# Last column loop: block 15 scored straight from PSUM with x weighted in advance, its last half block cut in two, and two middle half blocks summed by VectorE

## The chip, the cores and the metric

One core of one Trainium2 chip. The time is the device time of the whole program in microseconds (us). The kernel before was run three times; the trace that is read here is of one further, profiled execution.

## The reference, cut to what matters

For each of four batches, a long convolution over 12,608 positions and 128 channels (done here by matmul transforms) gives `y`, and `x * y` is the attention output. Then a top-k step replaces 128 rows of each batch:

```python
attn_out = x * y                                   # [4, 12608, 128]
scores = np.einsum('bsd,d->bs', attn_out, w_gate)
out = attn_out.copy()
for b in range(B):
    top_idx = np.argpartition(-scores[b], 128)[:128]
    xe = attn_out[b, top_idx]
    ye = np.maximum(xe @ w1, 0.0) @ w2
    g = 1 / (1 + np.exp(-scores[b, top_idx]))
    out[b, top_idx] = attn_out[b, top_idx] + g[:, None] * ye
```

So every row needs its product `x * y`, which goes to the output, and a score, the sum over 128 channels of that product times the gate vector `w_gate`.

## The kernel before, in words

Most of the program is a software pipeline over 128 groups (4 batches of 32), which transforms `u = x * v`, multiplies by the filter's spectrum and transforms half way back. What the change touches is the second half of the way back, the **column loop** `P1.run(ex)`, and only for the last batch, where nothing else is left in the pipeline (`ex` is set, `self.last` is true). For the other batches `P1` runs with `ex` empty.

A batch is 128 columns `j` of 128 rows by 128 channels. They are cut in 16 blocks of 8 columns, taken in the order `ORD` (0, 8, 1, 9, ... 7, 15), and each block in two half blocks of 4 columns: `hbs`, numbered `h` = 0 to 31. Half blocks 30 and 31 are block 15. Blocks 8 to 15 are called far here, the others near. For each `h` the loop emits

- `mm(h)`: the matmuls of its columns into one of three PSUM banks in turn (names `a`, `a`, `c` in the trace; lines 539 and 543). A bank can be written again when the half block three earlier has been read.
- `fin(h)`: VectorE multiplies the bank by `x` in SBUF, in place, into `xa` (line 554, 512 columns). Then the pending half block is weighted by the gate vector (`weigh`, line 589): near ones on VectorE, one half block later, with the gate vector held in PSUM; far ones on GpSimd at once (except `DW`). ScalarE sums the weighted products, one Copy with an accumulator for each column (`sums`, line 599). For `h` = 30 and 31 (`end`) VectorE does the scores itself with four multiply-and-accumulate operations (line 572), after the pending weighting.
- at the end of a block: the DMA of `xa` to the output (line 579; ScalarE's queue for the blocks at places 2 to 9 of the order, SyncE's for the others), a load of `x` for the block eight places on into the room of the block before (`load_a`, line 516, SyncE's queue, which must wait until that room's output DMA has landed; the load of block 15, at place 15, is emitted when the block at place 8, half blocks 16 and 17, is done), and after blocks 1 to 5 a `comb` on GpSimd (line 526), which prepares a near block's columns.

After the loop come the mask (line 603, VectorE) and the top-k of the last batch: 16 rounds, each of which counts on VectorE and ScalarE, adds up the counts with small matmuls (`total`, bf16, into a fourth bank) and makes a step on VectorE. The expert matmuls of the three other batches are woven in. `ex.start()`, emitted ahead of round 0, issues on TensorE in this order: the first half of an expert's first layer into the first bank of the ring (line 281, 16 rows in the trace), the second half into the second bank, and eight warming matmuls (line 811) into the third; on ScalarE a relu of the first half. Each engine runs its instructions in the order of emission.

Of the kernel before, what the change touches and what calls it, by code (L numbers as in the profile page):

```python
# [12 lines left out]
ALU = mybir.AluOpType  # L13
# [4 lines left out]
B, S, D, FO = 4, 12608, 128, 64  # L18
# [11 lines left out]
HB = 4  # L30
# [20 lines left out]
PC = 8  # L51
NL, NM = 28, 7
DW = (2, 14)
XI = 3
OFF, _o = {}, 0
for _n, _k, _w in (("te", 2, 2 * HC), ("qs", 2, HC), ("mt", 1, 2 * HC), ("ws", 1, 888), ("yz", 2, 2 * HC), ("sd", 2, 2 * HC),
# [5 lines left out]
CE = [o + 8 * D for o in XE]  # L62
XP = [OFF["wx"][0], *(OFF["xa"][0] + k * 8 * D for k in range(NX))]
XP[XI:XI] = XE
EARLY = [k for k in range(len(XP)) if not XI <= k < XI + 2]
KH = N1 // 2 + 1
# [113 lines left out]
def hyena_moe(ctx, tc, xg, x2, pos, bw, ww, wg, mw1, mw2, fo, fc, c1, gx, cf, ci, wm, tk, out):  # L180
    nc = tc.nc
# [6 lines left out]
    arena = cp.tile([128, ARENA], F32, name="arena")  # L188
    big = cp.tile([128, D * 2 * NJ + 4], F32, name="big")

    def view(t, off, shape):
        n = int(np.prod(shape[1:]))
        r = t[:shape[0], off:off + n]
        if len(shape) > 2:
            ax = "abcd"[:len(shape) - 1]
            r = r.rearrange(f"p ({' '.join(ax)}) -> p {' '.join(ax)}", **dict(zip(ax[1:], shape[2:])))
        return r
# [5 lines left out]
    def small(shape, name, dt=F32, tag=None):  # L203
        return sp.tile(shape, dt, tag=tag, name=name, bufs=2 if tag == "sc" else 1)
# [10 lines left out]
    def ps2(k, shape, name):  # L215
        return view(bank2[k], 0, shape)
# [18 lines left out]
    wgb = cp.tile([128, D + 4], F32, name="wgb")[:, 2:2 + D]  # L235
# [5 lines left out]
    junk = view(arena, OFF["cm"][0] + 2 * NC * D, [128, D])  # L241
# [25 lines left out]
    def stage_u(t):  # L267
        if t >= B * NG:
            return
        x, v = buf("x", t, [NP, XC]), buf("v", t, [NP, XC])  # L270
        nc.gpsimd.tensor_tensor(out=x, in0=x, in1=v, op=ALU.mult)  # L271
# [159 lines left out]
    def f_m(t, uv):  # L431
        ht = slots[:, t].rearrange("p (w c) -> p w c", w=2) if t < NG else buf("ht", t, [128, 2, HC])
        mt = buf("mt", t, [128, 2, HC])
        nc.vector.tensor_tensor(out=mt, in0=uv, in1=ht[:, 0].unsqueeze(1).to_broadcast([128, 2, HC]), op=ALU.mult)  # L434
        nc.vector.tensor_tensor(out=uv, in0=uv, in1=ht[:, 1].unsqueeze(1).to_broadcast([128, 2, HC]), op=ALU.mult)  # L435
        return mt

    def f_y(t, uv, mt):
        yz = buf("yz", t, [128, 2, HC])
        nc.vector.tensor_tensor(out=yz[:, 0], in0=uv[:, 1], in1=mt[:, 0], op=ALU.add)  # L440
        nc.vector.tensor_tensor(out=yz[:, 1], in0=mt[:, 1], in1=uv[:, 0], op=ALU.subtract)
        return yz
# [54 lines left out]
    hbs = [(ja, min(HB, z - ja)) for a, z in (blocks[k] for k in ORD) for ja in range(a, z, HB)]  # L497

    class P1:
        def __init__(self, b):  # L500
            self.b = b
            self.sc = small([128, NJ], f"sc_{b}", tag="sc")
            self.xa, self.s4, self.cm = {}, {}, {}
            self.mul = None
            self.hbs = hbs
            self.more = iter(CB)
            self.pw = self.nw = 0
            self.late = []
# [37 lines left out]
        def fin(self, h):  # L546
            ja, n = self.hbs[h]
            blk = ja // 8
            xa = self.xa[blk]
            js = slice(ja % 8, ja % 8 + n)  # L550
            end = self.last and h >= len(self.hbs) - 2
            if end:
                self.weigh()
            nc.vector.tensor_tensor(out=xa[:, js], in0=self.s4.pop(h)[:, :n], in1=xa[:, js], op=ALU.mult)
            if not end:
                self.weigh()
                far = ja >= JM and h + 1 < len(self.hbs) and h not in DW
                if h >= NL and not self.last:
                    o = OFF["cm"][0] + 2 * NC * D if h < 30 else OFF["wx"][0]
                    wx = view(arena, o + h % 2 * HB * D, [128, HB, D])  # L560
                elif far:
                    wx = view(arena, CE[self.pw % 2], [128, HB, D])
                    self.pw += 1
                else:
                    wx = self.wx[self.nw % len(self.wx)]
                    self.nw += 1
                self.mul = xa[:, js], wx[:, :n], ja, n, far, h
                if far:
                    self.weigh()
            else:  # L570
                for k in range(n):
                    nc.vector.scalar_tensor_tensor(out=junk, in0=xa[:, ja % 8 + k], scalar=1.0,
                                                   in1=self.wg, op0=ALU.mult, op1=ALU.mult,
                                                   accum_out=self.sc[:, ja + k:ja + k + 1])
            if ja + n == blocks[blk][1]:
                j0, j1 = blocks[blk]
                i = ORD.index(blk)
                eng = nc.scalar if 1 < i <= len(ORD) - len(XP) + 1 else nc.sync
                eng.dma_start(out[self.b, :, j0:j1], xa[P0:P0 + PR, :j1 - j0])
                if i:  # L580
                    self.load_a(i - 1 + len(XP))
                if blk in CB:
                    self.comb()

        def weigh(self):
            if self.mul:
                x, wx, ja, n, far, h = self.mul
                eng, w = (nc.gpsimd, wgb) if far else (nc.vector, self.wg)
                eng.tensor_tensor(out=wx, in0=x, in1=w.unsqueeze(1).to_broadcast([128, n, D]), op=ALU.mult)  # L589
                cols = [(wx[:, k], ja + k) for k in range(n)]  # L590
                if h < NL or self.last:
                    self.sums(cols)
                else:
                    self.late += cols
            self.mul = None
# [9 lines left out]
        def run(self, ex):  # L605
            self.last = ex is not None
            self.ring = (0, 1, 2) if ex else (3, 2, 0, 1)
            o = OFF["te"][0], OFF["ht"][0] + ((self.b + 1) * NG + 2) % NH * 2 * HC, OFF["x"][0] + (NU - 1) * XC
            if ex:
                o = OFF["te"][0] + 2 * HC, OFF["sd"][0], OFF["sd"][0] + 2 * HC  # L610
            self.wx = [view(arena, k, [128, HB, D]) for k in o]
            self.wg = ps2(1, [128, D], f"wg_{self.b}")
            nc.scalar.copy(out=self.wg, in_=wgb)
            for k in range(len(XE)):
                self.load_a(XI + k)
            for k in range(2):
                self.comb()
            for h in range(len(self.hbs)):
                self.mm(h)
                self.fin(h)  # L620
                if h == 29:
                    stage_u((self.b + 1) * NG + 5)
                if ex:
                    ex.hook(h, self.wg)
            self.weigh()
            if ex:
                self.mask()
# [465 lines left out]
    ex = None  # L1093
    bg = Background(iter(()))
    NT = B * NG
    for t in range(NT + LAG):
# [4 lines left out]
        if t < NT:  # L1101
# [19 lines left out]
            o = t - 1 in uv  # L1121
            if o:
                y = f_y(t - 1, uv[t - 1], f_m(t - 1, uv.pop(t - 1)))
# [23 lines left out]
        if t == NT:  # L1147
            bg.now = t
            bg.drain()
            ex = Experts(picked)  # L1150
# [8 lines left out]
        if i >= 0 and i % NG in LA:  # L1159
            if i % NG == LA[0]:  # L1160
                ph[b] = P1(b)
            k, e = divmod(LA.index(i % NG), 2)
# [39 lines left out]
def build(inputs):  # L1202
    import concourse.bacc as _bacc
    nc = _bacc.Bacc("TRN2", target_bir_lowering=False, num_devices=1, dynamic_dma_scratch_size=4096)
    arrays, args = {}, []
    for name, a in _layout(inputs):
        arrays[f"in_{name}_dram"] = a
        args.append(nc.dram_tensor(f"in_{name}_dram", a.shape, mybir.dt.from_np(a.dtype), kind="ExternalInput").ap())
    args.append(nc.dram_tensor("out_0_dram", (B, PR, NJ, D), F32, kind="ExternalOutput").ap())
    with tile.TileContext(nc) as tc:  # L1210
        hyena_moe(tc, *args)
    return nc, arrays
# [7 lines left out]
```

## Time and profile before

| | us |
|---|---|
| median of 3 runs | 829.29 |
| the runs | 828.87, 829.29, 840.53 |
| profiled execution | 828.99 |
| its span, first to last instruction | 827.2 |
| of it, the last column loop and the mask | 745.6 to 786.5 |
| 16 top-k rounds | 786.6 to 809.8 |
| selection, gather, last expert, scatter | 809.8 to 827.2 |

Busy shares over the whole span are TensorE 97%, VectorE 86%, GpSimd 79% and ScalarE 75%. They are means over stages with different limits; the change lies in one stage of some 40 us, so the stage is what is read. Times in the rows are us from the start of the span. A number in brackets at the end of a row is the idle time before it, with what ended it. Busy times of successive operations overlap a little, so the price of one is the distance between starts.

### The profile page before, as it was taken

Reading aid. Unit: us, or ns where it says so; the run is one execution under the profiler, and the core shown is the slowest. Engines: PE = TensorE matmul, PEld = TensorE weight load, DVE = VectorE, ACT = ScalarE, POOL = GpSimd, SP = SyncE. Lnnn points to the kernel's source line nnn. Section 1 sums busy time; section 2 is a strip of 40 time slices with the busy share of each in tenths; the row PEclk is TensorE's granted clock in tenths of the full one; section 3 lists DMA queues with packets and bytes.
Section 4 is the critical chain, followed back from the end, with each engine's and each line's share of the span. In section 5 each row is a group of like instructions: output and inputs, shape, how many; then the busy total and the mean of one; then the engine's idle time right before and its main releaser. Section 6 shows DMA issues by size and latency. Waiting matters only on the chain.

```text
span 827.2 us, 45233 instructions
## 1 busy us (share of the span) xinstructions
PE 802.9 (97%) x19216; PEld 675.9 (82%) x19216; DVE 712.4 (86%) x1402; ACT 616.7 (75%) x2273; POOL 654.9 (79%) x772
## 2 busy tenths in 40 slices
PE   9999999999999999999999999999999999999975
PEld 8989677777799777778998777778997777979864
DVE  7488899999899898999988989888989989997873
ACT  5366686555579898976599898856798989767971
POOL 5100499999998898999997999989988999989610
PEclk9999999999999999999999999999999999999996
DMA  8100577678969766787788666777797667846800
GB/s 285 43 2 2 186 222 220 219 244 273 290 207 346 246 213 208 231 271 260 229 289 319 216 213 203 254 232 241 250 328 243 218 213 231 268 148 208 321 29 7
DMA packets 77851, 178.41 MB, mean 216 GB/s; under 512 B 9104, under 2 KB 43897, under 8 KB 77649
## 3 DMA queue, kind: packets, MB, share of 16 engines
q1 hardware_dynamic: 73552, 161.23, 60.7%
q10 hardware_dynamic: 3840, 13.76, 4.9%
q8 instruction: 151, 2.47, 1.2%
q0 software_dynamic: 256, 0.52, 0.2%
q14 instruction: 52, 0.42, 0.1%
HBM read 135.77 MB, written 39.71 MB: 212 GB/s over the span
## 4 chain that ended last, share of the span: by engine, by line
PE 82%; DVE 5%; ACT 4%; DMA 2%; issue 2%; POOL 2%; SPq 1%; POOLq 0%; DVEq 0%; ACTq 0%
PE c L285 23%; PE a L420 18%; PE c L290 17%; PE a L539 6%; PE c L543 6%; PE c L539 3%; PE f L390 3%; PE a L374 3%; ACT arena L599 2%; PE f L356 2%; PE a L543 1%; DMA arena<-in_pos_dram 1%; PE a L356 1%; DMA arena<-hd 1%; DVE arena L434 1%
## 5 line engine op out<-in xcount | busy, mean ns | idle before, releaser
L285 PE MATMUL c<-ci_sb,arena 128*23 128x128 f32 x8128 | 249.2, 272 | 1.2 <-issue 0.6
L285 PEld LDWEIGHTS c<-ci_sb,arena 128*23 128x23 f32 x8128 | 226.6, 103 | 10.7 <-issue 2.5
L447 POOL TENSOR_TENSOR arena<-arena 128x364 f32<-128x364 f32 x127 | 113.8, 896 | 97.3 <-PE a L420 70.1
L290 PE MATMUL c<-arena,cf_sb 128*32 128x364 f32 x2048 | 185.5, 470 | 3.2 <-issue 1.5
L420 PE MATMUL a<-cons,arena 128*32 128x182 f32 (+1 forms) x4096 | 186.5, 318 | 1.2 <-POOL big L494 0.9
L420 PEld LDWEIGHTS a<-cons,arena 128*32 128x32 f32 (+1 forms) x4096 | 132.4, 110 | 50.3 <-issue 23.5
L599 ACT ACTIVATE arena<-arena 128x128 f32<-128x128 f32 x504 | 148.0, 299 | 9.7 <-DVE arena L589 9.2
L422 ACT COPY arena<-a 128x364 f32<-128x364 f32 x256 | 119.3, 466 | 43.7 <-PE a L420 39.3
L476 ACT COPY big<-c 128x768 f32<-128x768 f32 x127 | 100.2, 789 | 64.4 <-PE c L285 57.8
L271 POOL TENSOR_TENSOR arena<-arena 128x508 f32<-128x508 f32 x128 | 139.3, 1088 | 2.5 <-DMA arena<-in_xg_dram 2.5
L448 POOL TENSOR_TENSOR arena<-arena 128x364 f32<-128x364 f32 x127 | 114.3, 900 | 0.0
L290 PEld LDWEIGHTS c<-arena,cf_sb 128*32 128x32 f32 x2048 | 69.3, 110 | 48.6 <-issue 41.5
L599 ACT ACTIVATION_READ_ACCUMULATOR arena<-arena 128x1 f32 x504 | 96.2, 191 | 0.0
L429 DVE TENSOR_TENSOR c<-c,arena 128x364 f32<-128x364 f32 x128 | 69.6, 544 | 24.9 <-ACT arena L293 23.5
L434 DVE TENSOR_TENSOR arena<-c,arena 128x728 f32<-128x728 f32 x95 | 86.9, 914 | 2.8
L494 POOL TENSOR_TENSOR big<-big,arena 128x252 f32<-128x252 f32 x128 | 80.5, 629 | 10.0
L435 DVE TENSOR_TENSOR c<-c,arena 128x728 f32<-128x728 f32 x95 | 86.8, 914 | 0.0
L493 POOL TENSOR_TENSOR big<-big,arena 128x252 f32<-128x252 f32 x128 | 80.8, 632 | 1.0 <-ACT arena L477 1.0
L440 DVE TENSOR_TENSOR arena<-c,arena 128x364 f32<-128x364 f32 x127 | 68.2, 537 | 13.2 <-POOL arena L271 0.5
L293 ACT COPY arena<-c 128x364 f32<-128x364 f32 x128 | 59.2, 463 | 18.0 <-PE c L290 8.3
L426 DVE TENSOR_TENSOR c<-c,arena 128x364 f32<-128x364 f32 x128 | 69.6, 544 | 2.7
L526 POOL TENSOR_TENSOR arena<-big 128x512 f32<-128x512 f32 x56 | 70.3, 1281 | 0.7 <-PE c L539 0.6
(222 smaller groups left out, 1294.5 us busy)
## 6 DMA issues: line engine op xcount, KB each, us to landing
arena<-in_xg_dram SPq DMA_DIRECT2D x256, 254.0 KB, 3.3
arena<-hd SPq DMA_DIRECT2D x96, 364.0 KB, 4.2
arena<-in_x_dram SPq DMA_DIRECT2D x40, 420.0 KB, 6.2
out_dram<-arena SPq DMA_DIRECT2D x32, 420.0 KB, 5.8
out_dram<-arena ACTq DMA_DIRECT2D x32, 420.0 KB, 6.3
hd<-big SPq DMA_DIRECT2D x32, 364.0 KB, 3.8
arena<-in_x_dram SPq DMA_DIRECT2D x48, 210.0 KB, 4.5
arena<-in_pos_dram SPq DMA_DIRECT2D x8, 364.0 KB, 6.4
```

Of the source, the lines that this page charges most:

```text
L271: nc.gpsimd.tensor_tensor(out=x, in0=x, in1=v, op=ALU.mult)
L285: nc.tensor.matmul(o[32 * k:32 * k + c.stop - c.start], lhsT=lhsT[:, c], rhs=rhs, start=True, stop=True)
L290: nc.tensor.matmul(pq[a:a + 32, w], lhsT=cf_sb[:, 2 * w + a // NQ, a % NQ:a % NQ + 32], rhs=te[:, a // NQ], start=True, stop=True)
L420: nc.tensor.matmul(tps[s // 2][c, s % 2], lhsT=u[:, s, c], rhs=c1_sb[:, k], start=True, stop=True)
L422: nc.scalar.copy(out=te[:, :, 2 * h:2 * h + 2].rearrange("p e s i -> p s e i"), in_=tps[h])
L434: nc.vector.tensor_tensor(out=mt, in0=uv, in1=ht[:, 0].unsqueeze(1).to_broadcast([128, 2, HC]), op=ALU.mult)
L435: nc.vector.tensor_tensor(out=uv, in0=uv, in1=ht[:, 1].unsqueeze(1).to_broadcast([128, 2, HC]), op=ALU.mult)
L447: eng.tensor_tensor(out=nat(sd[:, 0]), in0=nat(yz[:, 0]), in1=rev(yz[:, 1]), op=ALU.add)
L448: eng.tensor_tensor(out=nat(sd[:, 1]), in0=rev(yz[:, 0]), in1=nat(yz[:, 1]), op=ALU.subtract)
L476: nc.scalar.copy(out=ay[:, t % NG, :NJ + JM, ss], in_=o3[:, :, :NJ + JM].rearrange("p s x -> p x s"))
L493: nc.gpsimd.tensor_tensor(out=d, in0=a, in1=s, op=ALU.subtract)
L599: nc.scalar.activation(out=x, in_=x, func=AF.Copy, accum_out=self.sc[:, j:j + 1])
```

## The change

It works on the last column loop alone (`ex` set).

- `hbs[-1]`, four columns, is cut in two half blocks of two columns, so that the loop has 33 half blocks, and 30, 31 and 32 are block 15.
- `ahead`: GpSimd multiplies `x` of half blocks 30, 31 and 32 by the gate vector, after `fin(25)`, `fin(26)` and `fin(27)`, into rooms of their own (`xw`).
- `fin` of 30 to 32: VectorE no longer multiplies into `xa`. It scores from PSUM, `sum(bank * xw)`, one operation for each column. ScalarE copies the bank to SBUF (`y`), GpSimd multiplies `y` by `x` into `xa`, and the output DMA follows.
- `DS`: for half blocks 17 and 21 (near) VectorE does the scores itself with four multiply-and-accumulate operations, in place of one weighting on VectorE and four sums on ScalarE.

```diff
+DS = (17, 21)
...
-            end = self.last and h >= len(self.hbs) - 2
+            end, ps = h in self.xw, self.s4.pop(h)[:, :n]
             if end:
                 self.weigh()
-            nc.vector.tensor_tensor(out=xa[:, js], in0=self.s4.pop(h)[:, :n], in1=xa[:, js], op=ALU.mult)
-            if not end:
+                for k in range(n):
+                    nc.vector.scalar_tensor_tensor(out=junk, in0=ps[:, k], scalar=1.0, in1=self.xw[h][:, k], op0=ALU.mult,
+                                                   op1=ALU.mult, accum_out=self.sc[:, ja + k:ja + k + 1])
+                y = self.ys[h]
+                nc.scalar.copy(out=y, in_=ps)
+                nc.gpsimd.tensor_tensor(out=xa[:, js], in0=y, in1=xa[:, js], op=ALU.mult)
+            else:
+                nc.vector.tensor_tensor(out=xa[:, js], in0=ps, in1=xa[:, js], op=ALU.mult)
+            if self.last and h in DS:
+                self.weigh()
+                for k in range(n):
+                    nc.vector.scalar_tensor_tensor(out=view(arena, OFF["v"][0] + 16, [128, D]), in0=xa[:, ja % 8 + k],
+                                                   scalar=1.0, in1=self.wg, op0=ALU.mult, op1=ALU.mult,
+                                                   accum_out=self.sc[:, ja + k:ja + k + 1])
+            elif not end:
                 self.weigh()
...
-            else:
-                for k in range(n):
-                    nc.vector.scalar_tensor_tensor(out=junk, in0=xa[:, ja % 8 + k], scalar=1.0,
-                                                   in1=self.wg, op0=ALU.mult, op1=ALU.mult,
-                                                   accum_out=self.sc[:, ja + k:ja + k + 1])
...
+        def ahead(self, h, o, y):
+            ja, n = self.hbs[h]
+            self.xw[h], self.ys[h] = (view(arena, a, [128, HB, D])[:, :n] for a in (o, y))
+            nc.gpsimd.tensor_tensor(out=self.xw[h], in0=self.xa[ja // 8][:, ja % 8:ja % 8 + n],
+                                    in1=wgb.unsqueeze(1).to_broadcast([128, n, D]), op=ALU.mult)
...
+            if ex:
+                ja, n = hbs[-1]
+                self.hbs = hbs[:-1] + [(ja, n // 2), (ja + n // 2, n - n // 2)]
+                v, y = OFF["v"][0] + 16, XP[0]
+                rooms = {25: (30, CE[1] + HB * D, y), 26: (31, v, y + HB * D), 27: (32, v + 2 * D, y + (HB + 2) * D)}
             for h in range(len(self.hbs)):
                 self.mm(h)
                 self.fin(h)
+                if ex and h in rooms:
+                    self.ahead(*rooms[h])
```

## Rows read from the trace of the kernel before

**Rows 1.** The chain that ended last, 700 to 830 us: start, length, what.
```profile
773.04 11.46 ACT arena L599 x79
...
784.57 1.65 ACT arena L599 x11
786.25 0.29 DVE sc L603
```

**Rows 2.** Timeline of TensorE: half block 21, half blocks 30 and 31, then the rounds.
```profile
770.09 1.04 PE L543 MATMUL a<-big,cons 128*64 128x128 f32 x16
...
780.13 1.92 PE L539 MATMUL a<-big,cons 128*64 128x128 f32 x32
782.94 1.09 PE L281 MATMUL a<-arena 128*64 128x128 f32 x16 [0.89 <-issue]
784.88 1.09 PE L281 MATMUL a<-arena 128*64 128x128 f32 x16 [0.85 <-DVE arena L554]
785.91 2.05 PE L811 MATMUL c<-ident 128*128 128x128 f32 x16
788.10 0.26 PE L281 MATMUL c<-st,onesb 128*64 128x3 bf16 x6
```

**Rows 3.** Timeline of VectorE: half blocks 18 and 21, then 28 to 31.
```profile
768.48 0.69 DVE L554 TENSOR_TENSOR arena<-a,arena 128x512 f32<-128x512 f32 x1
...
771.64 0.69 DVE L554 TENSOR_TENSOR arena<-a,arena 128x512 f32<-128x512 f32 x1 [0.64 <-PE a L539]
...
780.96 1.27 DVE L589 TENSOR_TENSOR arena<-arena,c 128x512 f32<-128x512 f32 x2
782.15 0.68 DVE L554 TENSOR_TENSOR arena<-a,arena 128x512 f32<-128x512 f32 x1
782.94 0.29 DVE L572 SCALAR_TENSOR_TENSOR arena<-arena,c 128x128 f32<-128x128 f32 x1
...
784.14 0.69 DVE L554 TENSOR_TENSOR arena<-a,arena 128x512 f32<-128x512 f32 x1
```

**Rows 4.** Timeline of GpSimd: the weightings of half blocks 22 and 23, 26 and 27.
```profile
774.41 2.16 POOL L589 TENSOR_TENSOR arena<-arena,wgb 128x512 f32<-128x512 f32 x2
778.16 2.26 POOL L589 TENSOR_TENSOR arena<-arena,wgb 128x512 f32<-128x512 f32 x2 [1.59 <-ACT arena L599]
```

**Rows 5.** Timeline of SyncE's queue, 773 to 775 us: the load of block 15.
```profile
773.88 0.33 SPq L516 DMA_DIRECT2D arena<-in_x_dram  x1
```

**Rows 6.** Operations on `in_x_dram`, 750 to 790 us: the eight loads of the loop, to landing.
```profile
DMA to landing us min/median/max: 4.4/6.2/7.9
```

**Rows 7.** Source line 516, 773.5 to 774.2 us: the load of block 15, to landing.
```profile
DMA to landing us min/median/max: 6.2/6.2/6.2
```

**Rows 8.** Timeline of all engines, 781 to 792 us: the first relu after the sums, rounds 0 and 1.
```profile
786.12 0.57 ACT L980 ACTIVATE arena<-a 128x512 f32<-128x512 f32 x1
...
788.40 0.16 DVE L728 SCALAR_TENSOR_TENSOR st<-c,cons 128x3 f32<-128x3 f32 x1 [0.21 <-PE c L281]
...
789.90 0.16 DVE L728 SCALAR_TENSOR_TENSOR st<-c,cons 128x3 f32<-128x3 f32 x1 [0.53 <-ACT arena L717]
```

**Rows 9.** Stretches of 1 us: length, busy us (count) of PE, PEld, DVE, ACT, POOL; granted clock; DMA share, GB/s.
```profile
804.00:805.00 1.00, 0.02 (x1) 0.00 (x0) 0.84 (x7) 0.80 (x3) 0.07 (x1) 0.89 0.19 66
...
812.00:813.00 1.00, 1.00 (x7) 0.98 (x8) 0.96 (x5) 0.00 (x0) 0.00 (x0) 0.50 0.00 0
...
818.00:819.00 1.00, 0.33 (x1) 0.14 (x1) 0.00 (x0) 0.23 (x1) 0.00 (x0) 0.78 0.00 0
...
825.00:826.00 1.00, 0.00 (x0) 0.00 (x0) 0.00 (x0) 0.00 (x0) 0.00 (x0) 0.63 0.19 66
```

**Rows 10.** Timeline of TensorE after 800 us: last dense matmuls ahead of a fall, warming at the half clock.
```profile
801.10 1.10 PE L281 MATMUL c<-arena 128*64 128x128 f32 x16
...
814.20 3.78 PE L811 MATMUL a<-ident 128*128 128x128 f32 x16
...
820.02 2.79 PE L281 MATMUL c<-arena 128*64 128x128 f32 x48
```

More of the change, by code (lines that the diff above doesn't have):

```diff
@@ L502, in __init__ @@
             self.sc = small([128, NJ], f"sc_{b}", tag="sc")
-            self.xa, self.s4, self.cm = {}, {}, {}
+            self.xa, self.s4, self.cm, self.ys = {}, {}, {}, {}
             self.mul = None
             self.hbs = hbs
+            self.xw = {}
             self.more = iter(CB)
```

## The prediction

> **What bounds the kernel now.** I read the chain of waits first, for the stretch that the change touches: it shows who hands over to the top-k. Up to about 773 us it runs through the column loop's matmuls, and from there on through ScalarE: 79 and then 11 rows of its sums, one after the other, until VectorE's mask starts at 786.25 [rows 1]. Each sum has two rows, so these 45 sums took 11.46 + 1.65 = 13.1 us, 0.29 each. Four sums are 1.17 us for a half block.
>
> Then each engine's timeline. VectorE ends its last score at almost the same moment: four scores start at 782.94 and the next product at 784.14, 0.30 a score, and four more follow the product of half block 31 [rows 3]. So two engines finish together, and a gain needs both to finish earlier. TensorE has ended the loop's matmuls long before, at 780.13 + 1.92 = 782.05. It then runs what `ex.start()` has put ahead of round 0, as its banks come free: one half layer at 782.94, as soon as VectorE's product of half block 30 has been read out (782.15 + 0.68), the second at 784.88 after the product of 31, then the warming matmuls [rows 2, 3]. These end at 785.91 + 2.05 = 787.96, and round 0's total starts at 788.10 [rows 2]. This is the row to keep in mind: TensorE reaches the first total 0.14 us before it is wanted. Whatever delays the two half layers delays the top-k one for one. What follows the second half layer takes 788.10 - 784.88 = 3.22, and the half layer itself 785.91 - 784.88 = 1.03; from the start of the first to the total it is 4.25 us without a hole.
>
> **The parts, and where each lies.**
>
> *Removed at the end.* VectorE loses the products of 30 and 31, at some 0.6 each (two operations of that width in 1.27, [rows 3]). The eight scores stay: still one operand in PSUM and one in SBUF, so I keep 0.3 each. Alone, this ends VectorE some 1.2 us earlier.
>
> *Half blocks 17 and 21.* ScalarE loses eight sums, 2.35 us. VectorE gets four scores (1.2) for one weighting (0.6) each time, but all four stand ahead of the next product. The product of 18 then moves from 768.48 to about 769.7 and ends at 770.4. TensorE needs the bank for half block 21 at 770.09 [rows 2], so it waits 0.35 us, and about 0.3 more at 25, after the scores of 21. VectorE has a hole of 0.64 us ahead of product 21 [rows 3], and one like it at each second near half block, which swallows the rest. The loop's matmuls end at 782.7 instead of 782.05, and VectorE's last score at about 785.45.
>
> *The weighting ahead on GpSimd.* Here the price is large. `ahead(30)` stands in GpSimd's queue after `fin(25)`, and behind it stand the weightings of 26 and 27, for whose results ScalarE waits. It reads `x` of block 15. That block's load is issued at 773.88 [rows 5], the last of eight on SyncE's queue, since it waits for room. It lands 6.2 us after its issue [rows 7]: at 780.1. Before, nobody wanted it ahead of 782.15. GpSimd has weighted 22 and 23 at 774.41 + 2.16 = 776.6 [rows 4], in the changed kernel some 0.7 later, at 777.3, and would then stand still for 2.8 us. The eight loads landed after 4.4 to 7.9 us [rows 6]; with the shortest it would still be 778.3, with the longest 781.8.
>
> From 780.1 on: `ahead(30)` 1.09 (half of the two in 2.16, [rows 4]), weighting 26 1.09, `ahead(31)` about 0.6 for half the width (an estimate from the same row), weighting 27 1.09, that is 784.0. Before, weighting 27 was through at 778.16 + 2.26 = 780.4 [rows 4]. ScalarE, which is through with 25 and 26 by then, does the sums of 27, 28 and 29 after it: 12 x 0.29 = 3.5, end at 787.5, where before it ended at 786.2. The eight sums saved are more than lost in waiting.
>
> *The copies on ScalarE.* The first, of bank 30, stands behind the sums of 29. It is as wide as the relu of 0.57 us [rows 8], also from PSUM, so it ends at 788.1. The next two are half as wide and hide behind the first half layer.
>
> *Who waits for them.* The half layers write the banks of 30 and 31, which are now free when ScalarE has copied them, no longer when VectorE has read them. The first starts at 788.15 instead of 782.94. Round 0's total follows 4.25 us later: 792.4 instead of 788.1, **+4.3**. The mask (787.6) and VectorE's 1.85 us from there to the counts (788.10 - 786.25) are hidden behind that. In round 1 VectorE waited 0.53 us for ScalarE, which was late by a relu [rows 8]; the relu is now done in time. That gives back between 0 and 0.53; I take 0.25, since part of the hole would be there anyway.
>
> *The clock.* TensorE now stands idle from 782.7 to 788.15, 5.4 us. Twice the trace shows the granted clock fall from 1.00 to 0.50 (2.4 to 1.2 GHz) after dense matmuls end: they end at 802.2 and the clock is down within 804 to 805, and they end at 822.8 and it is down within 825 to 826, 2.5 to 2.6 us later [rows 9, 10]. This gap is twice that, and nothing runs in it. At the half clock the 16 warming rows take 3.78 us instead of 2.05, 1.84 times as long [rows 2, 10]. The clock came back at about 818.4, some 6 us after the matmuls had become dense at 812 [rows 9]. So a fall costs between 0 (it doesn't come) and 4.25 x 0.84 = 3.6 us (the whole chain at the half clock). With 6 us at the half level it would be 6 x 0.46 = 2.8; the stretch after 812 was not without holes and the half layers are, so I take 5 us, **+2.3**.
>
> *Edits with no cost.* GpSimd's products for the output (1.09 and twice 0.6 after the copies) and the last output DMA move to about 790.5, and some 7 us of transfer follow. Behind them on GpSimd stands the first scatter (its turn came at 791.4 and shifts with the rounds), on SyncE nothing; the gather that reads the output comes after 815. One more half block is no more matmuls.
>
> **Sum.** Against the profiled execution of 828.99 (the median of the runs is 829.29, 0.3 more): 828.99 + 4.3 - 0.25 + 2.3 = **835.4 us**. The rounds and all that follows only shift.
>
> **The rivals.**
>
> 1. *The clock holds.* Everything else as above: 833.1. For it: only two falls are seen, and both were followed by thin or no work, so what comes after is not the same. Against it: 5.4 us idle. Chance 0.2.
> 2. *GpSimd isn't stopped by the load* (it lands by 777.3, against the shortest of eight). Then `ahead` fits in GpSimd's hole of 1.59 us [rows 4]. ScalarE still waits some 1.8 us for 18 and 22, since VectorE's four scores delay these products, and ends at 785.7 rather than 2.35 earlier; the first half layer starts at 786.25, the total 4.25 later, at 790.5: +2.4 - 0.25, so 831.1. With an idle TensorE of 3.5 us the clock may fall too, 833.4 then. Chance 0.15.
> 3. *Not slower: the change gives what it takes off VectorE and ScalarE.* The half layers would have to be out of the way, and the load in time. Then the mask starts at 785.75, 0.5 earlier, and with the 0.25 of round 1 it is 828.3. Against it: the matmuls that overwrite the banks have to wait for the copies, and the rows show no slack. It decides from a total wanted later than TensorE is ready. Chance 0.07.
> 4. *VectorE and GpSimd get in each other's way.* GpSimd's three products for the output, 2.3 us in all, now fall beside the mask and the first top-k operations, which have two inputs in SBUF. If such operations wait for each other, VectorE's counts come up to 2.3 us later. In the forecast this stays hidden: 787.6 + 1.85 + 2.3 = 791.8, ahead of TensorE's 792.4. Where TensorE is not the last (rival 3) it turns the gain into 828.3 + 2.3 = 830.6. No row shows such an operation beside a tensor operation of GpSimd. Chance 0.05. The Trainium skill (SBUF — State Buffer, section "SBUF: two separate sides") speaks for this rival: it calls the port pair that VectorE and GpSimd share "an exclusive lock, not a bandwidth split", which a VectorE operation with two SBUF inputs and a GpSimd operation can't hold together. No run here shows it yet.
>
> **How the numbers follow.** The forecast has 0.53. The range goes from 830.6 (rivals 2 and 4) to 836.8 (the forecast with the whole 3.6 for the clock); left out are rival 3 and some tail, about 0.15. A change of 2%, 16.6 us, is about what a measurement of this kernel can tell from none; none of the cases comes near it: faster 0.0, same 0.99, slower 0.01 for a collision that I haven't seen.
>
> **What would show it.** Right: GpSimd idle for 2 to 3 us ahead of `ahead(30)`, released by the load; ScalarE's sums end at about 787.5; the first half layer is released by ScalarE's copy at about 788; round 0's total starts at 792 to 796; a granted clock of 0.50 somewhere between 785 and 795. Wrong: GpSimd runs `ahead(30)` before 779, or the half layers start before the copies, or the clock stays at 1.00. The load is the step I am least sure of, since its landing moves with what the queues do.

## The result

The changed kernel takes **835.83 us** (median of 8 runs, 833.88 to 839.16), the kernel before, run beside it, 831.13 (8 runs). The ratio is **1.007, with a 95% interval of 1.0046 to 1.0094**: some 4 to 8 us slower. The forecast was 835.4, in a range of 830.6 to 836.8.

The profiled execution took 838.06 us, 9.1 more than the one of before. Not all of this need belong to the change: the column loop's first matmul starts at 750.11 us there and at 745.61 before, in code that is the same up to that point. The two rows are from the timelines of TensorE, before and after:

```profile
745.61 0.44 PE L539 MATMUL a<-big,cons 128*64 128x128 f32 x4 [0.61 <-ACT big L476]
```

```profile
750.11 0.44 PE L541 MATMUL a<-big,cons 128*64 128x128 f32 x4 [0.62 <-ACT big L477]
```

So in what follows every time is also given from the loop's first matmul on, written **L+**. Before, round 0's total comes at 788.10 - 745.61 = L+42.49, and the span ends at L+81.6; after, the total comes at 797.72 - 750.11 = **L+47.61** and the end at L+86.2. What the change costs in these two executions, 5.1 us, is all there at the first total, and 4.6 is left at the end.

The chain that ended last, 760 to 840 us, for the stretch of [rows 1]:

```profile
786.75 0.59 POOL arena L598
787.34 1.05 POOL arena L605
788.42 1.92 ACT arena L615 x13
...
790.68 1.35 ACT arena L615 x9
792.03 0.48 ACT arena L560
792.56 3.25 PE a L282 x32
795.81 1.98 PE c L834 x16
```

Before, it ran from ScalarE's sums to VectorE's mask. Now it begins on GpSimd (line 598 is `ahead`, 605 the weighting), goes on to ScalarE's last sums (615) and its copy of a bank (560), and from there to TensorE: the two half layers (282) and the warming (834). VectorE isn't on it any more. GpSimd's timeline, for [rows 4]:

```profile
779.84 2.15 POOL L605 TENSOR_TENSOR arena<-arena,wgb 128x512 f32<-128x512 f32 x2
784.61 1.09 POOL L598 TENSOR_TENSOR arena<-arena,wgb 128x512 f32<-128x512 f32 x1 [2.62 <-DMA arena<-in_x_dram]
785.66 1.09 POOL L605 TENSOR_TENSOR arena<-arena,wgb 128x512 f32<-128x512 f32 x1
786.71 0.64 POOL L598 TENSOR_TENSOR arena<-arena,wgb 128x256 f32<-128x256 f32 x1
787.30 1.09 POOL L605 TENSOR_TENSOR arena<-arena,wgb 128x512 f32<-128x512 f32 x1
```

`ahead(30)` waits 2.62 us for the load of `x`, and the two weightings stand behind it. TensorE's timeline, for [rows 2]:

```profile
792.56 3.25 PE L282 MATMUL a<-arena 128*64 128x128 f32 x32 [5.25 <-ACT arena L560]
795.74 2.05 PE L834 MATMUL c<-ident 128*128 128x128 f32 x16
797.72 0.26 PE L282 MATMUL c<-st,onesb 128*64 128x3 bf16 x6
```

An idle time of 5.25 us, ended by ScalarE's copy; the two half layers (32 rows) in 3.25 us. The granted clock in stretches of 1 us, as [rows 9]:

```profile
791.00:792.00 1.00, 0.00 (x0) 0.00 (x0) 0.00 (x0) 1.00 (x9) 0.00 (x0) 0.91 0.00 0
792.00:793.00 1.00, 0.44 (x4) 0.45 (x6) 0.88 (x4) 1.00 (x4) 0.36 (x1) 0.50 0.00 0
...
795.00:796.00 1.00, 1.00 (x14) 0.83 (x11) 0.51 (x5) 1.00 (x7) 0.32 (x1) 0.89 0.00 0
```

It falls to 0.50 shortly before the half layers begin and is back before the warming ends. Last, VectorE from the mask (line 619) on, with the wait of rounds 0 and 1, for [rows 8]:

```profile
792.07 0.29 DVE L619 TENSOR_TENSOR sc<-sc,cons 128x128 f32<-128x128 f32 x1 [1.83 <-ACT arena L615]
...
792.65 1.40 DVE L699 TENSOR_TENSOR sc<-sc,f 128x128 int32<-128x128 int32 x1
794.09 0.63 DVE L700 COPY hi<-sc 128x128 int16<-128x128 int16 x1
...
798.02 0.16 DVE L751 SCALAR_TENSOR_TENSOR st<-c,cons 128x3 f32<-128x3 f32 x1 [2.51 <-PE c L282]
...
799.27 0.16 DVE L751 SCALAR_TENSOR_TENSOR st<-c,cons 128x3 f32<-128x3 f32 x1 [0.28 <-PE c L282]
```

VectorE is done with its scores 1.83 us before ScalarE with the sums. Two of its operations (lines 699 and 700) take 1.40 and 0.63 us. Before, the same two were short:

```profile
786.84 0.29 DVE L676 TENSOR_TENSOR sc<-sc,f 128x128 int32<-128x128 int32 x1
787.17 0.23 DVE L677 COPY hi<-sc 128x128 int16<-128x128 int16 x1
```

Even so VectorE then waits 2.51 us for TensorE.

### The profile page after: what moved, and what is told of

Its sections match the earlier page's. It is cut to its first block, busy times and chain, and to the rows that moved or that the text cites. A ratio compares the mean times of both kernels' runs of the same rounds, so it can differ in the third digit from the quotient of the medians.

```text
span 836.3 us, 45243 instructions
## 1 busy us (share of the span) xinstructions
PE 805.1 (96%) x19216; PEld 687.1 (82%) x19216; DVE 713.7 (85%) x1414; ACT 616.9 (74%) x2260; POOL 661.6 (79%) x778
## 5 line engine op out<-in xcount | busy, mean ns | idle before, releaser
L286 PE MATMUL c<-ci_sb,arena 128*23 128x128 f32 (+1 forms) x8128 | 252.4, 272 | 3.6 <-issue 3.5
L286 PEld LDWEIGHTS c<-ci_sb,arena 128*23 128x23 f32 (+1 forms) x8128 | 229.4, 103 | 12.7 <-issue 6.1
L421 PE MATMUL a<-cons,arena 128*32 128x182 f32 (+1 forms) x4096 | 189.1, 318 | 2.6 <-issue 2.6
L291 PE MATMUL c<-arena,cf_sb 128*32 128x364 f32 x2048 | 188.2, 469 | 2.4 <-ACT arena L423 1.3
L421 PEld LDWEIGHTS a<-cons,arena 128*32 128x32 f32 (+1 forms) x4096 | 138.6, 110 | 46.2 <-issue 21.5
L615 ACT ACTIVATE arena<-arena 128x128 f32<-128x128 f32 x496 | 145.7, 296 | 12.7 <-DVE arena L605 9.4
L291 PEld LDWEIGHTS c<-arena,cf_sb 128*32 128x32 f32 x2048 | 74.9, 110 | 44.3 <-issue 36.4
L615 ACT ACTIVATION_READ_ACCUMULATOR arena<-arena 128x1 f32 x496 | 93.0, 188 | 0.0
```

Of the source, the lines that this page charges most:

```text
L286: nc.tensor.matmul(o[32 * k:32 * k + c.stop - c.start], lhsT=lhsT[:, c], rhs=rhs, start=True, stop=True)
L291: nc.tensor.matmul(pq[a:a + 32, w], lhsT=cf_sb[:, 2 * w + a // NQ, a % NQ:a % NQ + 32], rhs=te[:, a // NQ], start=True, stop=True)
L421: nc.tensor.matmul(tps[s // 2][c, s % 2], lhsT=u[:, s, c], rhs=c1_sb[:, k], start=True, stop=True)
L615: nc.scalar.activation(out=x, in_=x, func=AF.Copy, accum_out=self.sc[:, j:j + 1])
```

## The experiments

**The theory:** three steps in a row. GpSimd stands still until block 15's `x` has landed, so ScalarE gets its last products late; the half layers' banks are held by ScalarE's copies, which come after its last sums; in the gap TensorE's clock falls. **Rivals:** the four scores in the middle are what costs; VectorE and GpSimd get in each other's way; the changed program is slower ahead of the loop as well. All results are in one table, with L+ from the timeline of TensorE in each run's one profiled execution. Where only one execution was taken there is no ratio.

| run | loop starts | first half layer | round 0's total | end of span | ratio to before |
|---|---|---|---|---|---|
| before | 745.6 | L+37.3 | L+42.5 | L+81.6 | |
| before again (c1) | 748.0 | L+37.3 | L+42.5 | L+82.5 | |
| before, third (c2) | 748.1 | L+37.3 | L+43.9 | L+83.5 | |
| after | 750.1 | L+42.5 | L+47.6 | L+86.2 | 1.0070 (1.0046 to 1.0094) |
| after again (c3) | 758.3 | L+42.9 | L+48.9 | L+91.1 | |
| e1 middle only | 760.0 | L+38.1 | L+43.3 | L+82.2 | 1.0011 (0.9986 to 1.0036) |
| e2 end only | 748.9 | L+42.5 | L+47.8 | L+86.3 | 1.0072 (1.0045 to 1.0098) |
| e3 weighting ahead late | 753.5 | L+40.9 | L+46.3 | L+85.0 | 1.0064 (1.0036 to 1.0092) |
| e5 late, free banks | 746.4 | L+41.4 | L+46.6 | L+92.4 | 1.0140 (1.0107 to 1.0173) |
| e6 gap filled | 746.0 | L+42.2 | L+46.1 | L+88.4 | 1.0047 (1.0026 to 1.0068) |
| e7 no product | 754.6 | L+42.2 | L+47.7 | L+87.2 | |
| e8 late, own tile | 750.0 | L+39.4 | L+43.8 | L+84.5 | 1.0032 (0.9995 to 1.0070) |
| e9 product in rounds | 747.1 | L+39.4 | L+42.3 | L+82.9 | 1.0036 (1.0004 to 1.0068) |

**Is it the loop at all?** The kernel before twice more and the changed kernel once more, with no edit.

> The kernel before, unchanged. Theory (what comes ahead of the loop takes some us more or less from execution to execution, in code that the change doesn't touch): the loop's first matmul starts anywhere between 745 and 755 us, and from there round 0's total takes 42.5 us, as before, within 0.2. Rival (the changed program is slower ahead of the loop too): the loop starts at 745 to 746 us in every execution of this kernel.

> The kernel before once more, as the run before this one: a start of the loop between 745 and 755 us and 42.5 us to round 0's total, or, by the rival, a start at 745 to 746 us.

> The changed kernel, unchanged. Theory: the loop's first matmul starts anywhere between 745 and 755 us; from there round 0's total takes 47.6 us within 1 us (the fall of the clock comes at another moment), and from the loop's first matmul to the end of the span 86 us, within 3, where the kernel before took 81.6. Rival: the loop starts at 750 us or later again.

The kernel before starts its loop at 745.6, 748.0 and 748.1 us, and over all runs the start lies between 745.6 and 760.0: what comes ahead differs from execution to execution. The changed kernel's second start, 758.3, is later than expected and is what the rival said; against the rival stand four edits of the changed kernel that start between 746.0 and 748.9, and e1, in which this code is that of the kernel before, at 760.0. So few executions don't show that the changed program loses nothing ahead of the loop. The interval to the first total does tell: 42.5, 42.5 and 43.9 before, 47.6 and 48.9 after. Three figures missed what was expected: the 43.9, c3's 48.9, and c3's end at L+91.1. The 43.9 has its reason in the clock. TensorE's timeline of that execution (c2):

```profile
785.40 1.09 PE L281 MATMUL a<-arena 128*64 128x128 f32 x16 [0.89 <-issue]
787.35 1.82 PE L281 MATMUL a<-arena 128*64 128x128 f32 x16 [0.86 <-DVE arena L554]
789.10 2.93 PE L811 MATMUL c<-ident 128*128 128x128 f32 x16
791.96 0.26 PE L281 MATMUL c<-st,onesb 128*64 128x3 bf16 x6
```

And its clock, in stretches of 1 us (columns as in [rows 9]):

```profile
786.00:787.00 1.00, 0.49 (x10) 0.25 (x5) 0.93 (x7) 1.00 (x8) 0.00 (x0) 1.00 0.52 209
787.00:788.00 1.00, 0.65 (x8) 0.66 (x10) 0.90 (x6) 1.00 (x9) 0.00 (x0) 0.77 0.10 41
788.00:789.00 1.00, 1.00 (x12) 0.77 (x8) 0.86 (x6) 1.00 (x7) 0.00 (x0) 0.50 0.91 270
```

After two holes of 0.89 and 0.86 us the clock falls to 0.50, and the second half layer takes 1.82 instead of 1.09 us: the kernel before has such falls too, in one execution of three, and they cost it 1.4 us.

**The middle alone.** On the kernel before, half blocks 17 and 21 alone:

```diff
+DS = (17, 21)
...
-            if not end:
+            if self.last and h in DS:
+                self.weigh()
+                for k in range(n):
+                    nc.vector.scalar_tensor_tensor(out=view(arena, OFF["v"][0] + 16, [128, D]), in0=xa[:, ja % 8 + k],
+                                                   scalar=1.0, in1=self.wg, op0=ALU.mult, op1=ALU.mult,
+                                                   accum_out=self.sc[:, ja + k:ja + k + 1])
+            elif not end:
```

> Only half blocks 17 and 21 are scored by VectorE; the end of the loop is as before. Measured from the loop's first matmul to round 0's total, 42.5 us before and some 47.6 after. Theory (GpSimd stopped by the load, then banks held by ScalarE's copies, then the clock): the loop's matmuls and the last products are 0.65 us later and nothing else, 43.1 us, whole time +0.3 to +0.7. Rival (VectorE's four scores in the middle are what costs): 46 to 47.6, whole time +3 to +5.

L+43.25, 0.76 more than before, where 43.1 was expected; the loop's matmuls end 0.77 later (L+37.21 for L+36.44), and the whole time can't be told from before. The four scores delay what follows them a little and gain nothing. They don't explain 5 us.

**The end alone.** On the changed kernel, as all that follow:

```diff
-DS = (17, 21)
+DS = ()
```

> Only the end of the loop is changed; 17 and 21 are summed by ScalarE as before. Theory: GpSimd waits some 3 to 3.5 us for the load of block 15, ScalarE ends its sums where it does in the changed kernel, and the loop to round 0's total takes 46.7 to 48 us, whole time +4 to +6. Rival (the four scores in the middle): near 42.5, whole time within 1 us of before.

L+47.76: the whole loss, without the middle. Its rival falls.

**The weightings ahead at the end of GpSimd's queue.**

```diff
-                if ex and h in rooms:
-                    self.ahead(*rooms[h])
+                if ex and h == 27:
+                    for r in rooms.values():
+                        self.ahead(*r)
```

> The changed kernel with all three weightings ahead emitted after half block 27, so that nothing stands behind them on GpSimd but the products for the output. Theory: ScalarE's sums end 1.8 us earlier than in the changed kernel; the half layers still wait for ScalarE's copies, and round 0's total comes 44.9 us after the loop's first matmul at a granted clock of 1.00, up to 46.5 if it falls; whole time +2 to +4 against before. Rival (the stop of GpSimd costs nothing, the copies alone hold everything): 47.6, as in the changed kernel. Rival (the stop is all of it): 42 to 43.

The half layers start 1.6 us earlier (L+40.9 for 42.5), GpSimd no longer waits for the load. TensorE's timeline:

```profile
794.32 2.71 PE L282 MATMUL a<-arena 128*64 128x128 f32 x32 [3.66 <-ACT arena L560]
796.96 2.92 PE L835 MATMUL c<-ident 128*128 128x128 f32 x16
```

The total comes at L+46.3, the upper end of what was expected: the clock fell later, while the half layers ran (0.69 in the stretch 795 to 796), and stayed at 0.50 into the warming, which takes 2.92 us instead of 2.05. The whole time is 0.64% above before, some 5 us, where 2 to 4 were expected. So the stop is one step and not the whole.

**Other banks for the half layers, first try.** On top of the late weightings, the half layers go to the second banks of the two-bank PSUM tiles whose first banks hold half block 32 and the total, and the warming to the second bank of the gate vector's tile.

```diff
-            hp = ps1(f, [128, 4, CAP], f"mh_{f}")
+            hp = view(bank2[2 * f], 512, [128, 4, CAP])
```

> The one before, and the expert's half layers and the warming matmuls ahead of round 0 write PSUM banks that the column loop doesn't use. Theory: TensorE starts the half layers right after the loop and is ready ahead of the counts; VectorE's mask starts 0.5 us earlier than before; round 0's total comes after 42.0 us if VectorE's first operations aren't held by GpSimd's products, and after 43.5 if they are (the two operations after the mask took 1.40 and 0.63 us in the changed kernel, 0.29 and 0.23 before). Clock 1.00 up to the rounds, unless TensorE's short hole lets it fall. Whole time -0.8 to +1 against before. Rival (banks don't matter): as the run with late weightings.

A miss, and the slowest of all. Timeline of TensorE and of VectorE:

```profile
787.81 3.27 PE L282 MATMUL c<-arena 128*64 128x128 f32 x32 [4.20 <-ACT arena L560]
```

```profile
793.92 0.16 DVE L752 SCALAR_TENSOR_TENSOR st<-c,cons 128x3 f32<-128x3 f32 x1 [3.68 <-ACT arena L1009]
```

The half layers still wait for a copy, that of half block 32, and round 0's step on VectorE waits for ScalarE's relu of the other half layer: here the kernel's waits go by PSUM tile, not by bank, so two things in one tile wait for each other. The same happens in the rounds that follow (the end is at L+92.4). It doesn't tell the theory from its rival; the next but two does.

**The gap filled.** Eighteen warming matmuls more, ahead of the half layers, into the gate vector's tile:

```diff
+    def fill(n):
+        wp = view(bank2[1], 512, [128, 128])
+        for _ in range(n):
+            nc.tensor.matmul(wp, lhsT=ident, rhs=ident, start=True, stop=True)
...
         def start(self):
+            fill(18)
             self.step()
```

> The changed kernel with 18 more warming matmuls right after the loop's last ones, ahead of the expert's half layers, in a PSUM tile that the loop's matmuls don't use: some 4.6 us of work in the 5.3 us in which TensorE stood idle. Theory (the fall of the clock is the third step, and costs what the half layers show, 3.25 us instead of 2.06): granted clock 1.00 from the loop to the rounds, the half layers start where they did, 42.4 us after the loop's first matmul, and round 0's total comes after 46.7 instead of 47.6; whole time 0.9 us less than the changed kernel. Rival (the half layers are slow for another reason, their operands or banks): 3.25 us again, total after 47.6.

Timeline of TensorE:

```profile
783.48 4.29 PE L834 MATMUL c<-ident 128*128 128x128 f32 x36 [0.24 <-DVE arena L605]
788.26 1.97 PE L282 MATMUL a<-arena 128*64 128x128 f32 x32 [0.50 <-ACT arena L560]
790.16 2.05 PE L839 MATMUL c<-ident 128*128 128x128 f32 x16
792.14 0.26 PE L282 MATMUL c<-st,onesb 128*64 128x3 bf16 x6
```

The half layers take 1.97 us instead of 3.25, and the chain from their start to the total is 792.14 - 788.26 = 3.88 us, its price at the full clock. The total is at L+46.1. The clock is the third step, shown by taking it away. The end is no better: in this execution the clock fell again in round 8 (half layers of 2.00 and 1.81 us there), after a hole of 1.60 us on TensorE. The kernel before has that hole too, of 1.60 us in c1, with the clock at 1.00 behind it; whether the filling has a part in this fall isn't shown. The whole time is 0.26 to 0.68% above before, and that it is better than the changed kernel's 0.46 to 0.94% isn't shown either, since the intervals overlap.

**No products for the output on GpSimd.** The products of the last half blocks are left out; a copy of one column stands in for each:

```diff
-                nc.gpsimd.tensor_tensor(out=xa[:, js], in0=y, in1=xa[:, js], op=ALU.mult)
+                nc.gpsimd.tensor_copy(xa[:, ja % 8:ja % 8 + 1, :1], y[:, :1, :1])
```

> The changed kernel without GpSimd's products for the output of block 15 (their place is taken by a copy of one element each, so this block's output stays x). Theory (GpSimd and VectorE exclude each other there, but hidden behind TensorE): the two VectorE operations after the mask take 0.29 and 0.23 us again instead of 1.40 and 0.63, and round 0's total still comes 47 to 48 us after the loop's first matmul. Rival (the exclusion is what delays round 0): total 1.5 us earlier, 46.1. Rival (the two operations are long for another reason): 1.40 and 0.63 again.

VectorE's timeline:

```profile
796.92 0.32 DVE L699 TENSOR_TENSOR sc<-sc,f 128x128 int32<-128x128 int32 x1
797.27 0.23 DVE L700 COPY hi<-sc 128x128 int16<-128x128 int16 x1
...
802.62 0.16 DVE L751 SCALAR_TENSOR_TENSOR st<-c,cons 128x3 f32<-128x3 f32 x1 [4.32 <-PE c L282]
```

0.32 and 0.23 us again, and no gain: VectorE waits 4.32 us for TensorE instead of 2.51. So GpSimd's products do hold VectorE up, by 1.5 us, and this is hidden in the changed kernel.

**A tile of their own for the half layers.** With late weightings, the first expert's half layers and the warming, now ahead of them, in the gate vector's tile, which nobody needs after half block 29. The relu of the first half layer is now emitted behind the second half layer.

```diff
-            hp = ps1(f, [128, 4, CAP], f"mh_{f}")
+            hp = view(bank2[1], 512 * f, [128, 4, CAP]) if own else ps1(f, [128, 4, CAP], f"mh_{f}")
```

> The changed kernel with the three weightings ahead emitted after half block 27, and the first expert's two half layers and the eight warming matmuls (now ahead of them) in the PSUM tile that held the gate vector, which neither the last banks nor the total use; the run with free banks had them in tiles shared with both. Theory: the half layers no longer wait for ScalarE's copies, TensorE is through 41.4 us after the loop's first matmul, and the total waits for VectorE's counts, which GpSimd's products hold up by 1.5 us: 43.7; whole time +0.5 to +1.5 against before. Rival (something else than the copies gates TensorE): 45 to 46.5 as with late weightings alone.

Timelines of TensorE and of VectorE:

```profile
789.43 1.97 PE L282 MATMUL c<-arena 128*64 128x128 f32 x32
793.77 0.26 PE L282 MATMUL c<-st,onesb 128*64 128x3 bf16 x6 [2.37 <-DVE arena L731]
```

```profile
790.42 0.29 DVE L619 TENSOR_TENSOR sc<-sc,cons 128x128 f32<-128x128 f32 x1 [0.28 <-ACT arena L615]
...
791.00 1.39 DVE L700 TENSOR_TENSOR sc<-sc,f 128x128 int32<-128x128 int32 x1
792.43 0.63 DVE L701 COPY hi<-sc 128x128 int16<-128x128 int16 x1
```

As forecast: TensorE is ready 2.37 us early and waits for VectorE, whose two operations are long; L+43.75 where 43.7 was expected. Behind that wait the clock falls (0.58 in the stretch 794 to 795, then 0.50), round 0's half layer takes 1.75 us, and from the total to the end it is 40.7 us, where it was 38.6 in the changed kernel: so part of what is won at the total is lost again, and the end is at L+84.5.

**And the products on VectorE, in the rounds.**

```diff
-                nc.scalar.copy(out=y, in_=ps)
-                nc.gpsimd.tensor_tensor(out=xa[:, js], in0=y, in1=xa[:, js], op=ALU.mult)
+                for k in range(0, n, 2):
+                    self.tail.append((xa[:, ja % 8 + k:ja % 8 + k + 2], ps[:, k:k + 2]))
...
                 self.counts(r)
+                if self.ex and self.p1.tail:
+                    o, ps = self.p1.tail.pop(0)
+                    nc.vector.tensor_tensor(out=o, in0=ps, in1=o, op=ALU.mult)
```

> The one before, and block 15's products for the output go to VectorE, straight from PSUM, a half of a half block in each of rounds 0 to 3, in place of ScalarE's copies and GpSimd's products. Theory: nothing holds VectorE's first operations any more (0.29 and 0.23 us), total 42.2 us after the loop's first matmul, where it was 42.5 before; each product costs some 0.1 us more than VectorE's wait in its round. Whole time between -0.6 and +0.3 against before: no difference that can be measured. Rival (the change's scores from PSUM have a price of their own): 43.5 or more.

VectorE's timeline:

```profile
788.09 0.29 DVE L704 TENSOR_TENSOR sc<-sc,f 128x128 int32<-128x128 int32 x1
788.41 0.23 DVE L705 COPY hi<-sc 128x128 int16<-128x128 int16 x1
...
789.35 0.42 DVE L779 TENSOR_TENSOR arena<-c,arena 128x256 f32<-128x256 f32 x1
```

0.29 and 0.23 us; the total starts at L+42.26, 0.23 ahead of before, and that is all that the scores from PSUM are worth there. Not even this is kept, as TensorE's timeline shows:

```profile
789.35 0.23 PE L282 MATMUL c<-st,onesb 128*64 128x3 bf16 x4 [0.87 <-DVE arena L735]
789.83 0.19 PE L282 MATMUL c<-st,onesb 128*64 128x1 bf16 x2 [0.26 <-ACT arena L727]
```

The total's last two rows wait for ScalarE's count, which stands behind the relu that was moved, and VectorE's step on the total starts at L+42.98, where it was L+42.79 before. Each of the four products in the rounds takes 0.42 us, and by round 3 VectorE's step is 1.0 us behind that of before. The end is at L+82.9, within the three of before. The ratio, 1.0036 with an interval that begins at 1.0004, is no gain, and some 3 us more than before where at most 0.3 was expected: no version here beats the kernel before.

## Why the prediction was right, and where it failed

The ladder at the start of the first total, from these runs. The rows of e3 and of the changed kernel are worked out: the measured start of the half layers plus 3.88 us, the chain of half layers and warming at the full clock (e6). The prices hold in this order only, since a wait that a longer one covers costs nothing by itself (e7).

| from | to | adds, us |
|---|---|---|
| before, 42.49 | scores from PSUM and the middle, nothing in the way (e9), 42.26 | -0.23 |
| e9 | products on GpSimd beside VectorE (e8), 43.75 | +1.49 |
| e8 | banks held by the copies (e3: 40.86 + 3.88 = 44.74) | +0.99 |
| e3 | GpSimd stopped by the load (after: 42.45 + 3.88 = 46.33) | +1.59 |
| at the full clock | as it was, 47.61 | +1.28 |

- **The load.** It was to land at 780.1. With the loop's start of before, GpSimd went on at 784.61 - 4.50 = 780.1; it waited 2.62 us (2.8 were forecast). ScalarE's sums were to end at 787.5; the mask that waits for them started at 792.07 - 4.50 = 787.57. Right, and shown by e3.
- **The copies hold the banks.** First half layer at 788.15 forecast, 792.56 - 4.50 = 788.06 measured, released by ScalarE's copy. Right; e8 shows it by taking it away.
- **The chain to the total** was put at 4.25 us, the distance of the rows in the kernel before. Run in one go it is 3.88.
- **The clock** is the term of the sum that was mis-sized: +2.3, from 5 us at the half clock. In the profiled execution the half layers start at 792.56, and the clock is back at about 795.2 (an estimate from the 0.89 of the stretch 795 to 796): 2.7 us, not 5, and the price is 47.61 - 46.33 = 1.3. In the second execution it is 48.91 - 42.89 - 3.88 = 2.1, in e2 and e7, by the same working, 1.4 and 1.6. All are below 2.3; and the kernel before pays 1.4 in one execution of three, which the sum didn't count. Mechanism right, term too large: the clock came back sooner than in the row that the term was taken from (some 6 us), and why isn't shown.
- **Round 1** gives back 0.25: VectorE's steps of rounds 0 and 1 stand 1.25 us apart, 1.50 before [rows 8]. Right.
- **Rival 4** is real but hidden, as the prediction had it: 1.5 us, where 2.3 was the bound. The Trainium skill (SBUF — State Buffer, section "SBUF: two separate sides") has the rule, an exclusive lock on a shared port pair; e7 agrees (1.40 and 0.63 us with GpSimd's products, 0.32 and 0.23 without).
- **The middle** was to delay TensorE by 0.65 us; it did by 0.76.
- **The step that failed** is the one from the sum to the chances: "A change of 2%, 16.6 us, is about what a measurement of this kernel can tell from none", and with it the 0.99 on no change. No row was given for the 2%. With 8 runs of each the interval is 0.24% to either side, and a loss of 0.7% stands clear of it; so did the sum's own 6.4 us, 0.8%, which the chances called nothing.
- **The sum** had the direction right and the size too large, by the clock above all: to the first total it has 4.3 + 2.3 = 6.6 us for 5.1 measured; of the 1.5 between them the clock is 1.0 and the chain 0.4. To the end the change costs 4.6 us in the profiled execution, and the medians differ by 4.7, not 6.4. That 835.4 met 835.83 is partly luck: the base was one execution of 828.99 us, 2.1 below the kernel before's median of 831.13 in 8 runs, and this made up for the 1.7 too much.

What stays open is how often the clock falls in the rounds and what that costs to the end: L+81.6 to 83.5 before, 86.2 and 91.1 after, with different falls in each. In c3, for one, the clock is at 0.50 in round 8 (820 to 822 us) and in the last expert's matmuls (840 to 843), where the profiled execution of the changed kernel has 1.00. How much of the 4.7 us between the medians lies ahead of the loop is open too.

## What to carry to other kernels

Work moved ahead in an in-order queue waits for its own inputs, and everything behind it waits too: look up when the data land, not only when they used to be needed. When a reader of a PSUM bank is replaced by a slower one on a busy engine, ask who writes that bank next. And an engine that is ready 0.14 us ahead of its turn has no cover to give.

## What the runs showed that was not expected

- A wait between VectorE and GpSimd shows as a longer VectorE operation (0.29 to 1.40 us, 0.23 to 0.63), not as idle time in front of it.
- In one execution of the kernel before (c2) the granted clock fell to 0.50 after two holes of 0.89 and 0.86 us about a half layer of 1.09. The same holes left it at 1.00 in two other executions.
- Banks of one PSUM tile were not independent here: matmuls and a VectorE step waited up to 4.20 us for ScalarE's work in the tile's other bank (e5).
